# Windowed attention of layer B: from products on VectorE to small matmuls on TensorE, with a new instruction order

## Chip, core and metric

The kernel runs on one core of a Trainium2 chip. Engines: PE (TensorE: matmuls and transposes; its weight loads are shown apart as PEld), DVE (VectorE), ACT (ScalarE), POOL (GpSimd) and SP (SyncE, whose queue issues nearly all transfers). Each engine works through its own instructions in program order and waits for others by semaphores. The metric is the device time of one execution in microseconds, the median of several runs.

## Reference

Four residual layers, A, B, A, B, on 2,048 tokens of width 512, with 32 heads of 16 channels. Layer A is a linear attention with a softmax feature map and isn't changed in what it computes. Layer B is attention over a window: a token attends to itself and to the seven tokens 2, 4, ... 14 places before it.

```python
W, dil = 8, 2
...
pos = jnp.arange(S)
off = jnp.arange(W) * dil
idx = pos[:, None] - off[None, :]
mask = idx >= 0
...
logits = jnp.einsum("bhsd,bhswd->bhsw", q, kg) * scale
logits = jnp.where(mask[None, None, :, :], logits, -1e9)
attn = _softmax(logits, axis=-1)
o = jnp.einsum("bhsw,bhswd->bhsd", attn, vg)
...
x = x + _A_ref(_layernorm(x, axis=-1), A_wqkv, A_w_phi, A_wo)
x = x + _B_ref(_layernorm(x, axis=-1), B_wqkv, B_wo)
x = x + _A_ref(_layernorm(x, axis=-1), A_wqkv, A_w_phi, A_wo)
x = x + _B_ref(_layernorm(x, axis=-1), B_wqkv, B_wo)
```

## The kernel before

**Tiling.** Tokens are cut into four blocks b of 512, each of four tiles t of 128; x stays in the SBUF. Weights are loaded once. A step name says its stage: a1 (keys and values of layer A, and the sum kv over all tokens), a2 (queries), a3 and a4 (denominators, the output of layer A and its projection `s_out`), b1 (Q, K, V of layer B), b2 (scores and softmax), b3 (values, then `s_out`). L is 0 for the first pair of layers and 1 for the second. kv joins all four blocks, so a3 of a layer starts after a1 of all of them.

**Order.** Each stage registers its steps in threads, one for each engine. The text `_ORDER` lists the order in which the steps are issued, for all engines together. `_CHOICE` holds one bit for each eviction (`flex`): DVE (L190) or ACT (L192). In `s_out` the bit also says how x is added: by one more matmul with the identity on PE (L523) and a copy on ACT (L530), or by an addition on DVE (L533). `_SLOTS` gives each tile its buffer. A queue never passes a step that waits.

**Layer B.** b1 makes Q, K and V transposed, channels on partitions (the 384 matmuls of L927), with 16 columns of the block before in front of K and V (copies on POOL). `prod` (L1019, DVE) multiplies Q by the eight shifted windows of K, four times 128x4096 a block; `lgt` (L1026, PE) adds the products of a head with a 0/1 matrix on 128x32 tiles of the array, so that heads and offsets lie on partitions. Exponentials are on ACT (L1033), denominators are matmuls (`den`, L1042) with ln and exp on ACT (L1047, L1049), and DVE multiplies (`PT`, L1054). `vrep` (L988, SP) spreads V over the partitions, 16 transfers a block. `pav` (L1081, DVE) multiplies probabilities by values, four times 128x4096 a block, and `mo` (L1090, PE) adds up the eight offsets with another 0/1 matrix; the result leaves by L190/L192 as oT, and `s_out` (L520) projects it.

**Other lines of the prediction.** L540: squares for the layernorm (ACT). L460 and L451: transposes of the normalized x on PE and by DMA. L668: kv of layer A (128x33 tiles of the array, 64 columns). L714 and L782: sums and denominators of layer A (128x32 tiles, 128 columns). L808 and L816: broadcast of the factors and the multiplication. L900: output of layer A (32x32 tiles, 512 columns). L242 and L252: clearing a constant and building PHI at the start, L493: the first layernorm's statistics.

Of the kernel before, what the change touches and what calls it, by code (L numbers as in the profile page):

```python
# [16 lines left out]
P = 128  # L17
# [12 lines left out]
KVW = 16 + TB  # L30
VGW = 3 * KVW + TB + 8
# [5 lines left out]
_BUFS = {"big": 8, "med": 16, "t2": 6, "ps": 8}  # L37
# [3 lines left out]
    "fold_dma": (),  # L41
    "half_k": ((0, 3), (1, 3)),
    "half_ln": (),
    "split": ((1, 2), (1, 3)),
    "v_dram": (),
    "half_mo": (),
    "rho_pad": 0,
# [10 lines left out]
av 8 i i i i i i i i i i i i 0 f 0 g e 2t 0 bs 9 h a d c 0 j k t i i j l 27 o p 3 3 d6 b 1x 1x t 1y o m 2 2 1q  # L58
1z 1x 1x q u t r 1q v x w n s 1r w 1s 4 20 y 21 1x 22 1x 23 1q 1q 1q 1q 1v 1w z 3d 3d 3d 1u 1t 25 3e 3e 3e z 5
3e 3e z z 26 10 18 18 d5 1 z 16 11 4i 15 6 1h 13 3d 3e 3e 25 25 26 18 25 18 12 26 26 28 26 26 26 26 19 12 28  # L60
2a 28 1h 18 14 12 12 1a 28 1c 3e 2g 2g 1f 2h 2h 1h 1h 1b 1i 2b 1b 1e 1d 29 2j 2k 1h 1j 1n 2r 1b 1l 2s 1b 2c 2r
1k 2s 17 2g 2g 2h 2h 1k 1k 2h 2h 2h 2h 2d 1g 2d 2d 2d 2e 2j 1m 35 36 32 2o 2o 33 2s 33 32 33 33 2r 2s 2s 1o 2o
2o 2d 2r 3a 1k 3a 1p 2p 2o 24 24 2s 24 2u 2v 35 37 2u 2u 2u 2s 2i 2w 2j 3a 2s 3a 2l 2z 2j 24 32 32 34 2m 3b 33
3d 3f 3f 2z 2z 2z 33 2f 33 33 2f 2f 2f 3a 3a 2q 2q 2q 30 3a 2n 3a 3a 2z 3e 2q 2x 35 35 b6 3b 3a 2y 31 31 31 31
3c 3c 38 3c 39 3c 3m 3f 3n 3o 3o 3o 24 24 3g 3g 3g 3f 3p 3q 3g 3g 3g 3g 3g 3r 3q 3f 3g 24 3h 3i 3i 5l 5m 5n 3p
3s 3q 3j 3k 3k 3t 3q 3p 3x 5m 3w 3u 3h 3i 3i 3q 3v 3q 3q 3y 3h 3i 3q 3i 3h 3i 3q 5l 5o 5p 5r 5m 5q 7 7 3z 3q
3i 3j 3k 5m 5l 5s 3k 7 7 5m 5m 5m 3h 3i 7g 40 5u 44 41 42 5t 5m 5m 3j 3j 7h 7i 3k 5v 5m 5w 43 7h 45 7j 45 60
3k 3k 3k 46 45 45 5y 5x 5z 61 61 48 47 47 61 49 47 4a 47 4b 62 47 4b 63 3j 4g 94 4c 45 4d 45 4e 4f 3k 45 45 61
64 63 4h 4p 65 95 7j 7j 66 4q 63 96 95 97 97 63 67 7h 63 67 69 7h 6b 4k 4k 4k 4l 4p 4r 4k 4m 4p 4p 4s 4t 7k 7n
6a 68 6c 4o 7m 50 50 4u 4u 4u 4n 4u 7l 4w 97 7o 7p 7p 7q 7s 3l 4x 7r 7r 7p 7t 7p 6o 7u 50 7r 7r 7v 6o 6j 4v 4y  # L70
4j 6o 6q 6o 4j 4z 6k 6p 6r 6j 7r 6e 6l 95 6d 95 7v 6t 6s 6f 6d 7w 6e 7z 7x 98 9b 9a 99 6g 7y 9c 6e 6j 6j 9d 9d
6u 9d 6e 6n 80 6m 9d 6h 6v 6v 9e 9h 9f 6i 9g 9f 6w 6v 6v 6w 6w 9f 9i 9f 87 88 8h 9j 9f 50 82 9j 9l 6w 6x 6x 87
87 6w 81 83 9n 6x 9k 87 8b 89 51 51 51 51 52 52 8c 8c 8e 6u 6u 6u 9m 8j 8a 8d 8c 6v 6y 3l 8f 82 9o 82 85 82 50
51 52 4z 4z 4z 9q 9q 9s 8c 6z 8g 6y 6z 9r 71 70 6y 6y 6z 6z 72 86 a0 a0 a1 73 84 8i 74 75 74 74 50 74 8i 76 8i
77 a2 76 79 53 53 54 55 54 a5 56 53 54 9v 78 76 9q 9q 76 a0 81 53 9v 9w 9p 7a 57 9v 9u a7 76 7a 9t 8j 7c 9y 54
58 59 59 59 9v 59 9x 7d 7e 5a 8j 8j 7b 7f 5c 5b 5d 5b 5b a0 8k 5e 5b 5f 8k 9z a7 5b 5f 5j 8k 8k 8l a3 5i b4 a4
b7 5h b4 b4 b4 8l 5g b5 b5 a7 b5 b5 a7 8k 8l 8j c3 8i c3 b8 c4 c4 c4 c4 a8 8m a8 a8 a8 c3 a9 a9 5k at c1 b5 a6
8m au au c1 c2 b5 c2 aw c2 c2 a8 a9 b5 b5 8n 8o 8n 8p 8m at au at at 8n 8q 8m a7 aa 8n aw 8r 8s au au au 8s 8s
8t au au 8s 8v a6 a6 8u aa 8w aa 8x 8u 8u 8u 8y ab ac ab ad a6 aa b7 8u b9 b7 c3 8y 90 92 c1 91 c1 c2 8z c2 c2
aw ay ab c2 ba ae ab af aw b0 c4 c4 b1 bc ag ag ag ag ah bc aj ak bc c1 c4 c4 bc al ax c3 ai ai ai bd b1 ai am  # L80
93 bf bi bg az bf ai am ar bf bf bg bg aq b7 bg bg bg bg bg bb an ao ag ag ap bi ag ag b1 b1 bc b2 c2 bi bn bi
bl bk as bq br br bq br br bq bq b1 br by by by by bt b3 b3 b3 b3 br be be be br br bz c5 c5 bh bj bn bn bn c5
bu c4 by by by by c6 bo by c6 c6 c5 bt bt bt bn bv c6 c6 c6 bz be bp bp bw bm bp bp c0 c0 by c6 c6 bx c0 c0 c9
c5 ca c6 cb cb cc cb cd ce cd fr fs c7 c8 c7 c8 c8 ft cc ci cf cd cg cd c7 c8 c8 fs fu c8 e2 fu ch cd e3 cd cc
cj ck e4 cd c7 c8 c8 c7 e3 e2 cm cd c8 e6 e7 fu cl cd cd cn cp co e5 e3 hb e3 cr e2 ea e9 cq hc cs e3 cs e8 e3
e3 hd eb ec e3 e3 e3 ed ct cv hc eh cs he ee cs ef cw eg ei cx ei ei cu ei cu cu cu fs cy fs fv ej cu cy d0 cz
ek d2 fw fx fz d3 cs cs fy cs cs g0 g0 g0 el ek em ek en ek d4 d1 dc g1 eo ek g2 g3 g2 dc de eo es g0 g4 dd dh
g2 g5 g2 he hc eq g6 d7 d8 d7 d7 d7 he di dc g2 dc d9 ep er hc et dn hf da db df dh dh dh hi hh hj hg hk hk hk
dj dk dl dm dm g6 g7 g9 dn dn dg ga f0 f0 hl hm hn hm ho hm ev ew f1 hk dn g8 do do hp f2 fa fc hm hq do do dp
ev ex fc gb ev f0 dp ey dn f3 f0 hm fc f4 hq ev ez fc do dp dn dq dq d6 f5 f6 dm dm eu hs gi gj gi fd gs hr fd  # L90
ht fd hu hv fd dq fe fe f5 f5 f8 f5 f9 f7 fb gk fd fe fc gn gn gp gi gi gl gm gd gd gd ge ic gf i7 i7 i9 gg i8
dr dr dt ds dr du hx hy gd dq gu dr dv gn gq gh i7 ff ia gu fb go ff fg fh fb fb eu gv gc gn i2 gr i3 hx hz hx
i7 i2 ib gv i4 hx i1 gc hw i2 i2 i5 gu i0 gu gv gv gw gt ie fg fi if i6 ie id gw if dw dx id gv gw id id ie ie
if if ig dw ff ig if ig fg fj dw e0 dw ff fg fk ie fl fm fl fn gu fl fl fp ih ih ih ih e1 ii ii ii ik ij fq dy
gt gt gt fo fo il io io io io ii im ip iq ip is ir ir ih ii in ip ip iu it ir gx ir gy gx gx gx gz gy h0 dz dz
iv gy h1 h4 gx gy h2 h4 iw iv h5 h5 h6 h7 gy h4 h3 h5 h8 h9 h7 h7 h4 h5 ha h7
# [4 lines left out]
    "0011111111111001110111111010000010010000000000000001011111101100100000110101000110000010000001110111"  # L101
    "1101011110010000110101000000000000001101011000000000100100000000000000000101111100000011011000000000"
    "0000000000001101111010000000100101011111010000011001110111000000000000000111111011101110010100101000"
    "00000000000001111001000000000000000000000000000000000000000000000000000000000001111"
# [3 lines left out]
_SLOTS = {  # L108
    "big": (
        "0123456701231231456204632073205712053720457604356704213560421356720415763215063506432506"  # L110
    ),
    "med": (
        "0123456789abcdef5837ae98eeaeae471853bc9e43cbe47199ce3185413cebf94c8f74e3581bc71931bc7f370bf9ac21584e"
        "af9c37214a0b589dec37"
    ),
    "t2": (
        "0123450123450342150132451032451032451032451302153421530421503452014520345123045130425123504321504321"
        "5043215043210451023134"
    ),
    "ps": (  # L120
        "0123456701234750613250746132074365462150743510635127035164051362731405263710452763210743562107423251"
        "0764376215043762435107625407152367423167052341760543210675432170652147053624036542076314257603415203"
        "6415026734107534105234065265346053460562036207346201542015471204712603712035764120356471032516407324"
        "6735012463754021637261350247613025476130746513072463501742635017463015276301562703152760432764327014"
        "6570324650324705613245076"
# [4 lines left out]
class _Fast:  # L130

    def __init__(self, ctx, tc, A_x, A_wqkv, A_w_phi, A_wo, B_wqkv, B_wo, out):
        self.tc, self.nc = tc, tc.nc
        self.out = out
        e = ctx.enter_context
        self.const = e(tc.tile_pool(name="const", bufs=1))
        self.bigp = e(tc.tile_pool(name="bigp", bufs=1))
        self.medp = e(tc.tile_pool(name="medp", bufs=1))
        self.t2p = e(tc.tile_pool(name="t2p", bufs=1))
        self.small = e(tc.tile_pool(name="small", bufs=2))  # L140
# [7 lines left out]
        self.ntile = {t: 0 for t in _BUFS}  # L148
        for n in ("xn", "xnT", "oT", "Eq", "rS", "kvp", "K", "QT", "Vg", "PT", "vh"):
            setattr(self, n, {})  # L150
# [7 lines left out]
    def ps(self, dt=F32):  # L158
        return self.psp.tile([P, 2048 // (4 if dt == F32 else 2)], dt, name="ps", tag=self.slot("ps"))
# [35 lines left out]
    def constants(self):  # L195
        nc, const = self.nc, self.const
        self.ident = ident = const.tile([P, P], BF16, name="ident")
# [1620 lines left out]
```

## Time and profile before

| What | Value |
|---|---|
| Median of 3 runs | 329.83 us (329.33 to 331.2) |
| Span of the profiled execution | 327.5 us, 8033 instructions, granted TensorE clock 0.998 |
| PE busy | 310.3 us (95%), 3176 matmul records |
| DVE busy | 302.2 us (92%), 439 instructions |
| ACT busy | 279.3 us (85%), 634 instructions |
| POOL busy | 25.3 us (8%) |
| DMA | 35.41 MB; the hardware queue 53.6% of 16 engines' span |

The span goes from the first instruction to the last of one profiled execution; the page gives no other time for it, and the runs' median is 2.3 us above it. Busy time is the time in which at least one instruction of the engine is under way: instructions overlap at their ends, on ACT and DVE by some 90 ns each, so sums of mean durations exceed it. [...] A few matmul records are missing (234 of 256 of L520 with 128x128 tiles are there, for instance). In a group of the lines view stand: line, engine, operation, output and inputs, shapes and count; then busy us and mean ns of one; then idle time before it and what ended it.

### The profile page before, as it was taken

How to read it: one execution, taken by the hardware profiler on the slowest of the kernel's cores; microseconds unless marked ns; L12 is line 12 of the kernel's file. 1: busy time of each engine (PE TensorE's matmuls, PEld its weight loads, DVE VectorE, ACT ScalarE, POOL GpSimd, SP SyncE). 2: the span in 40 equal slices, each digit the busy share in tenths (PEclk: the TensorE clock that was granted, in tenths of full speed). 3: DMA queues.
4: the chain of work that ended last, by engine and by line, in shares of the span. 5: the costliest groups of instructions: out<-in, count | busy, mean ns of one | idle time of the engine just before them, and what ended most of it. 6: DMA issues, size and time to landing. Idle time of an engine off the chain costs nothing. (4 is left out here: it accounts for less than half of the span.)

```text
span 327.5 us, 8033 instructions
## 1 busy us (share of the span) xinstructions
PE 310.3 (95%) x3176; PEld 149.5 (46%) x3203; DVE 302.2 (92%) x439; ACT 279.3 (85%) x634; POOL 25.3 (8%) x50
## 2 busy tenths in 40 slices
PE   7999999999999999999999999979999999999873
PEld 3655456445444444443444455644544454433221
DVE  7998995998998999899999999699999999999993
ACT  5999988998888999989999999798999996676550
POOL 4000000000021003000000000000000208400000
PEclk9999999999999999999999999999999999999999
DMA  7980000004556899998750300023436977679952
GB/s 197 380 197 3 0 2 4 2 20 120 105 148 135 152 164 133 139 121 154 137 135 1 67 3 2 4 59 90 128 58 125 179 146 134 150 139 158 166 176 92
DMA packets 37388, 35.41 MB, mean 108 GB/s; under 512 B 23008, under 2 KB 32224, under 8 KB 37344
## 3 DMA queue, kind: packets, MB, share of 16 engines
q1 hardware_dynamic: 36816, 34.81, 53.6%
q8 instruction: 27, 0.44, 0.6%
q14 instruction: 17, 0.14, 0.2%
q10 hardware_dynamic: 528, 0.02, 0.1%
HBM read 10.50 MB, written 2.36 MB: 39 GB/s over the span
## 5 line engine op out<-in xcount | busy, mean ns | idle before, releaser
L927 PE MATMUL ps<-xnT,WB 128*128 128x512 bf16 x384 | 87.6, 380 | 0.5 <-DMA xnT<-xn 0.5
L1081 DVE TENSOR_TENSOR pav<-PT,Vg 128x4096 bf16<-128x4096 bf16 (+1 forms) x34 | 72.0, 2162 | 1.5 <-DMA Vg<-V 1.0
L1019 DVE TENSOR_TENSOR prod<-QT,K 128x4096 bf16<-128x4096 bf16 x32 | 72.5, 2291 | 0.3 <-ACT QT L192 0.2
L927 PEld LDWEIGHTS <-WB 128*128 128x128 bf16 x384 | 42.3, 114 | 43.3 <-issue 5.8
L520 PEld LDWEIGHTS <-oT 128*128 128x128 bf16 x256 | 23.8, 97 | 34.5 <-ACT oT L192 5.7
L192 ACT CAST oT<-ps 128x512 bf16<-128x512 f32 (+1 forms) x60 | 32.1, 587 | 8.4 <-PE ps L1090 7.1
L706 ACT ACTIVATE Eq<-ps 128x512 bf16<-128x512 f32 x64 | 34.0, 615 | 0.7 <-PE ps L698 0.6
L520 PE MATMUL ps<-WoB,oT 128*128 128x512 bf16 x122 | 32.1, 380 | 2.4 <-ACT oT L192 2.0
L599 ACT ACTIVATE Ek<-ps 128x512 bf16<-128x512 f32 x64 | 33.6, 622 | 0.4 <-PE ps L593 0.2
L698 PE MATMUL ps<-xnT,WA 128*128 128x512 bf16 x128 | 30.7, 380 | 0.6 <-DVE Eq L816 0.6
L540 ACT ACTIVATE sqd<-x 128x512 bf16<-128x512 bf16 x48 | 30.1, 643 | 1.0 <-DVE x L533 0.8
L605 PE MATMUL ps<-WA,xnT 128*128 128x512 bf16 x120 | 30.0, 380 | 0.5 <-issue 0.2
L593 PE MATMUL ps<-WA,xnT 128*128 128x512 bf16 x124 | 29.7, 380 | 0.6 <-DMA xnT<-xn 0.2
L520 PE MATMUL ps<-WoA,oT 128*128 128x512 bf16 x120 | 29.2, 380 | 0.4
L533 DVE SCALAR_TENSOR_TENSOR x<-ps,x 128x512 bf16<-128x512 f32 x38 | 25.4, 686 | 1.9 <-PE ps L520 1.7
L192 ACT CAST V<-ps 128x512 bf16<-128x512 f32 x31 | 17.5, 595 | 4.4 <-PE ps L927 4.3
L192 ACT CAST K<-ps 128x512 bf16<-128x512 f32 x31 | 17.8, 585 | 3.7 <-PE ps L927 3.3
L530 ACT ACTIVATE x<-ps 128x512 bf16<-128x512 f32 x26 | 15.1, 598 | 6.4 <-PE ps L523 6.3
L192 ACT CAST QT<-ps 128x512 bf16<-128x512 f32 x29 | 17.1, 592 | 2.5 <-PE ps L927 2.5
L651 DVE TENSOR_TENSOR Ek<-Ek,rk 128x4096 bf16<-128x4096 bf16 (+1 forms) x10 | 18.6, 1858 | 0.5 <-ACT rk L646 0.5
L593 PEld LDWEIGHTS <-xnT 128*128 128x128 bf16 x128 | 12.1, 97 | 15.4 <-DMA xnT<-xn 0.7
L446 ACT ACTIVATE xn<-x,nmr,rstd 128x512 bf16<-128x512 bf16 x23 | 18.2, 822 | 1.0 <-DVE nmr L435 0.8
(129 smaller groups left out, 433.3 us busy)
## 6 DMA issues: line engine op xcount, KB each, us to landing
Vg<-V SPq DMA_DIRECT2D x128, 131.5 KB, 4.4
Prho<-rd SPq DMA_DIRECT2D x8, 512.0 KB
x<-in_A_x_dram SPq DMA_DIRECT2D x3, 512.0 KB
WB<-in_B_wqkv_dram SPq DMA_DIRECT2D x3, 512.0 KB, 11.6
wraw<-in_A_wqkv_dram SPq DMA_DIRECT2D x4, 256.0 KB, 4.5
out_dram<-x SPq DMA_DIRECT2D x4, 256.0 KB, 2.2
out_dram<-x SPq DMA_DIRECT2D x8, 128.0 KB, 2.2
x<-in_A_x_dram SPq DMA_DIRECT2D x4, 128.0 KB
```

Source lines behind the costliest of these rows:

```text
L192: self.nc.scalar.copy(out=out, in_=in_)
L520: nc.tensor.matmul(y[:], lhsT=oT[:, c, t * P:(t + 1) * P], rhs=Wo()[:, c, :], start=(c == 0), stop=(c == NB - 1 and not onpe))
L533: nc.vector.scalar_tensor_tensor(out=xb[:, t, :], in0=T[t][:], scalar=1.0, in1=xb[:, t, :], op0=ALU.mult, op1=ALU.add, **kw)
L540: nc.scalar.activation(out=sqd[:], in_=xb[:, t, :], func=ACT.Square, accum_out=T["ss"][:, t:t + 1])
L593: nc.tensor.matmul(pk[:], lhsT=xnT[:, t, k, :], rhs=self.WA[:, k, D:2 * D], start=(k == 0), stop=(k == NB - 1))
L599: nc.scalar.activation(out=T["E"][:, t, s, :], in_=T["k", t][:], func=ACT.Exp, scale=1.0 - 2.0 * s)
L605: nc.tensor.matmul(pv[:], lhsT=xnT[:, t, k, :], rhs=self.WA[:, k, 2 * D:3 * D], start=(k == 0), stop=(k == NB - 1))
L698: nc.tensor.matmul(pq[:], lhsT=self.WA[:, k, hb * P:(hb + 1) * P], rhs=xnT[:, :, k, :], start=(k == 0), stop=(k == NB - 1))
L706: nc.scalar.activation(out=self.Eq[L, b][s][:, :, hb, :], in_=T[hb][:].rearrange("p (t i) -> p t i", t=4), func=ACT.Exp, scale=1.0 - 2.0 * s)
L927: nc.tensor.matmul(pp[:], lhsT=self.WB[:, k, i * D + c:(i + 1) * D:NB], rhs=xnT[:, :, k, :], start=(k == 0), stop=(k == NB - 1))
L1019: nc.vector.tensor_tensor(out=pr[:], in0=QT[:, c:c + 1, :].to_broadcast([P, NW, TB]), in1=win, op=ALU.mult)
L1081: nc.vector.tensor_tensor(out=pv, in0=PT[:, :, lo:lo + n].unsqueeze(1).to_broadcast([P, NB, 2, n]), in1=vw, op=ALU.mult)
```

## The change

Layer B is computed in another way; layer A keeps its operations, some of them twice as wide.

- *Tokens* are laid out anew in x: a block's tile t holds tokens of one parity (r = t // 2), so that the window is eight neighbours. Loads and stores of x follow.
- *b1* keeps its 384 matmuls: Q and K transposed as before, V with tokens on partitions. Q is copied by eight transfers a block (`qsc`) into `Qbd`, which holds, for each group of four heads, a block diagonal with zeros elsewhere. V goes with a column of ones into `Vs`, is written to DRAM (`vwr`, 2 a block) and read back (`vrd`, 8 a block) into `Vbd`, block diagonal too. `Qbd` and `Vbd` exist once; their zeros are set at the start by DVE.
- *b2*, for each tile of 128 tokens: scores of 32 keys against 40 queries for four heads at once, on 64x32 tiles of the array; exponential of 640 elements twice; a band mask on DVE.
- *b3*, for each tile: probabilities as weights, values as moving data (68 columns: four heads of 16 and a one), 32 matmuls and 32 for the keys of the group of 32 before; ln and exp of the denominator on ACT; the division by DVE straight from PSUM.
- *b4*: the output is transposed, by DMA for blocks 0 to 2 and on PE for block 3, then `s_out`.
- PSUM is one tile of eight banks; `pp` takes two neighbouring banks. Exponentials of a1 and a2, the evictions of a4 and the multiplication of a3 work on two banks at a time. ln and exp that were one step are two.
- `_ORDER`, `_CHOICE` and `_SLOTS` are new throughout: 1551 steps instead of 1452. 3 residual additions are done by the identity on PE instead of 26. Unused options are gone.

```diff
+WN = 40
+DV = DH + 1
...
+    "ob_dma": {(0, 0): 4, (0, 1): 4, (0, 2): 4, (1, 0): 4, (1, 1): 4, (1, 2): 4},
...
     def ps(self, dt=F32):
-        return self.psp.tile([P, 2048 // (4 if dt == F32 else 2)], dt, name="ps", tag=self.slot("ps"))
+        bank = self.PS[:, int(self.slot("ps")[2:]), :]
+        return bank if dt == F32 else bank.bitcast(dt)
+
+    def pp(self):
+        k = int(self.slot("pp")[2:])
+        return self.PS[:, k:k + 2, :]
...
+        self.Qbd = const.tile([P, NB, NB, TB], BF16, name="Qbd")
+        self.Vbd = const.tile([P, 2, 9, NB, 8 * DV], BF16, name="Vbd")
...
+        def zero_q(i):
+            nc.vector.memset(self.Qbd[:, 2 * i:2 * i + 2, :, :], 0.0)
+
+        def zero_v(i):
+            nc.vector.memset(self.Vbd[:, i // 2, 5 * (i % 2):5 + 4 * (i % 2), :, :], 0.0)
...
-        for b in range(1, 4):
-            add("ld_x%d" % b, "SP", lx, b)
+        for b in range(1, 4):
+            for r in range(2):
+                add("ld_x%d" % b, "SP", lx, b, r)
...
-            nc.scalar.activation(out=T["E"][:, t, s, :], in_=T["k", t][:], func=ACT.Exp, scale=1.0 - 2.0 * s)
+            nc.scalar.activation(out=T["E"][:, 2 * t:2 * t + 2, s, :], in_=T["k", t][:], func=ACT.Exp,
+                                 scale=1.0 - 2.0 * s)
...
+        def mv(t):
+            xnT = self.xnT["B%d" % L, b]
+            T[2, t] = pp = self.ps()
+            for k in range(NB):
+                nc.tensor.matmul(pp[:], lhsT=xnT[:, t, k, :],
+                                 rhs=self.WB[:, k, 2 * D:3 * D],
+                                 start=(k == 0), stop=(k == NB - 1))
...
+        def qsc(g):
+            lo = DH * g
+            nc.sync.dma_start(out=self.Qbd[lo:lo + DH, :, g % 4, :], in_=T[0][lo:lo + DH, :, :])
...
+        def vrd(r, c):
+            j = 0 if b else 1
+            src = self.VD[L][r, 256 * b - 32 + 32 * j:256 * b + 256, c * 8 * DV:(c + 1) * 8 * DV]
+            nc.sync.dma_start(out=self.Vbd[32 * c:32 * c + 32, r, j:9, c, :],
+                              in_=src.rearrange("(j k) e -> k j e", k=32))
...
+        def mm(S, r, c, s, n, pos, K, k0, q0):
+            o = S[32 * c:32 * c + 32, r, s * 160 + pos:s * 160 + pos + 1]
+            out = bass.AP(o.tensor, o.offset, [list(o.ap[0]), [WN, NB], [1, n]])
+            nc.tensor.matmul(out, lhsT=K[64 * r:64 * r + 64, c, k0:k0 + 32],
+                             rhs=Q[64 * r:64 * r + 64, c, :, q0:q0 + n],
+                             start=(s == 0 and pos == 0), stop=(s == 1), tile_position=(64 * r, 32 * c),
+                             skip_group_check=True)
+
+        def sc(f):
+            S = T[f] = self.pp()
+            K = self.K[L, b]
+            for s in range(2):
+                k0 = t * P + 64 * f + 32 * s
+                for c in range(NB):
+                    for r in range(2):
+                        mm(S, r, c, s, 32 if f and s else WN, 0, K, k0, k0)
+            if f == 0:
                 return
...
+            for c in range(NB):
+                for r in range(2):
+                    mm(S, r, c, 1, 8, 32, Kp, k0, t * P)
+
+        def ex(f):
...
+            nc.scalar.activation(out=E, in_=T[f][:, :, 0:320], func=ACT.Exp, scale=float(DH) ** -0.5,
+                                 accum_out=self.stE[:, 2 * idx + f:2 * idx + f + 1])
+
+        def msk():
+            E = self.ET[L, b, t][:].rearrange("p r s h q -> p (r s h) q")
+            nc.vector.tensor_tensor(out=E, in0=E, in1=self.maskW[:].unsqueeze(1).to_broadcast([P, 32, WN]),
+                                    op=ALU.mult)
...
+        def pv(e, s, n, ks, pos):
+            j = 4 * (t % 2) + 1 + s - (pos > 0)
+            v = V[:, t // 2, j, 0, DV * e:DV * e + 1]
+            rhs = bass.AP(v.tensor, v.offset, [list(v.ap[0]), [8 * DV, NB], [1, DV]])
+            nc.tensor.matmul(T["O"][32 * s:32 * s + n, e, 0:NB * DV],
+                             lhsT=self.ET[L, b, t][:, e // 4, ks, e % 4, pos:pos + n], rhs=rhs,
+                             start=(e % 4 == 0 and pos == 0), stop=(pos > 0),
+                             tile_position=(0, 32 * s), skip_group_check=True)
+
+        def mo():
+            T["O"] = self.pp().rearrange("p o (e x) -> p (o e) x", x=P)
+            for e in range(8):
+                for s in range(4):
+                    pv(e, s, 32, s, 0)
+            for e in range(8):
+                for s in range(4):
+                    if s or t % 2 or b:
+                        pv(e, s, 8, (s + 3) % 4, 32)
...
+        def ln():
+            T["r"] = self.sm([8, NB], "rdB")
+            den = T["O"][:, :, 0:NB * DV].rearrange("p e (c d) -> p e c d", d=DV)[:, :, :, DH]
+            nc.scalar.activation(out=T["r"][:], in_=den, func=ACT.Ln, bias=self.tiny_t[:, 0:1])
+
+        def rd():
+            nc.scalar.activation(out=T["r"][:], in_=T["r"][:], func=ACT.Exp, scale=-1.0,
+                                 accum_out=self.stR[:, idx:idx + 1])
+
+        def nrm():
...
+            nc.vector.tensor_tensor(out=out, in0=num, in1=T["r"][:].unsqueeze(3).to_broadcast([P, 8, NB, DH]),
+                                    op=ALU.mult)
...
+        def tr(lo, n):
+            nc.sync.dma_start_transpose(
+                out=tile()[:, lo:lo + n, :, :].rearrange("k t c p -> k (t c) p"),
+                in_=self.oB[L, b][:, lo:lo + n, :].rearrange("p t d -> p (t d)"))
```

In the new list DVE begins with kvT, maskH, PHI, half of Qbd's zeros, the small constants, indAV, a quarter of Vbd's zeros and indB, and then the statistics of the first two tiles.

More of the change, by code (lines that the diff above doesn't have):

```diff
@@ L63 @@
[L63 to L67, printed above, removed]
@@ L126 @@
+    "et": (
+        "01234560231460512436015263142501"
     ),
@@ L275, in ind_b @@
                 in_=self.indAV[:].rearrange("p (a h) -> p a h", h=8).unsqueeze(3).to_broadcast([P, NB, 8, DH]))
-        def ind_den():
-            nc.vector.tensor_copy(out=self.indDen[:],
-                                  in_=self.indAV[:].unsqueeze(1).to_broadcast([P, NB, H]))
-        for f in (zero, small, mask_h, phi, ind_s, mask_2, ind_qk, ind_av, ind_b, ind_den):
+        for f in (zero, small, mask_h, phi, ind_s, mask_2, ind_av, ind_b, mask_w):
             add("c_" + f.__name__, "DVE", f)
+        for i in range(2):
+            add("c_zq%d" % i, "DVE", zero_q, i)
+        for i in range(4):
+            add("c_zv%d" % i, "DVE", zero_v, i)
         def warm():
@@ L572, in s_out @@
                 add(st, "ACT", sq, t)
-                if half and t % 2:
-                    norm(t - 1, 2)
             elif last and split:
@@ L578, in s_out @@
                 add(st, "SP", store, t - 1, t + 1)
-        if not last and not half:
+        if not last:
             norm(0, 4)
@@ L640, in t1, with rl @@
                                     op=ALU.add)
+        def rl(t, m):
+            s1 = T["s1"][:, 0:m * G]
+            nc.scalar.activation(out=s1, in_=s1, func=ACT.Ln)
         def rr(t, m):
@@ L990, in s_b1 @@
-        if b:
-            add(st + "v", "POOL", vhalo_in)
-        else:
-            add(st + "k", "POOL", kzero)
-            add(st + "v", "POOL", vzero)
-        for i in range(3):
-            for c in range(NB):
-                add(st + "qkv"[i], "PE", mm, i, c)
-                self.flex(st + "qkv"[i], ev, i, c)
-        if b:
-            add(st + "kh", "POOL", halo)
-        if b < 3:
-            add(st + "v", "POOL", vhalo_out)
-        if (L, b) in _OPT["v_dram"]:
-            add(st + "v", "SP", vwr)
@@ new lines, in vrd @@
+        def vrd(r, c):
[3 more added lines that the diff above has]
+                              in_=src.rearrange("(j k) e -> k j e", k=32))
+        for i in range(2):
+            for c in range(NB):
+                add(st + "qk"[i], "PE", mm, i, c)
+                self.flex(st + "qk"[i], ev, i, c)
+        for g in range(8):
+            add(st + "q", "SP", qsc, g)
@@ new lines, in s_b3 @@
+    def s_b3(self, L, b, t):
+        nc, add = self.nc, self.step
+        st = "b3_%d%d%d" % (L, b, t)
+        key = "A%d" % (L + 1)
+        idx = (L * 4 + b) * 4 + t
+        T = {}
+        V = self.Vbd
+        def pv(e, s, n, ks, pos):
[23 more added lines that the diff above has]
+        def nrm():
+            if (L, b) not in self.oB:
+                self.oB[L, b] = self.med([4, D], "oB")
+            num = T["O"][:, :, 0:NB * DV].rearrange("p e (c d) -> p e c d", d=DV)[:, :, :, 0:DH]
+            out = self.oB[L, b][:, t, :].rearrange("p (c e d) -> p e c d", c=NB, d=DH)
+            nc.vector.tensor_tensor(out=out, in0=num, in1=T["r"][:].unsqueeze(3).to_broadcast([P, 8, NB, DH]),
+                                    op=ALU.mult)
+        add(st, "PE", mo)
+        add(st, "ACT", ln)
+        add(st, "ACT", rd)
+        add(st, "DVE", nrm)
```

566 lines of the change are left out of this document (234 added, 332 removed).

## The prediction

> **What bounds the kernel now.** I read the windows view first (busy time of each engine in stretches of 20 us), to see who is full where.
>
> ```profile
> 100.00:120.00 20.00, 19.95 (x166) 9.04 (x167) 19.38 (x20) 18.03 (x45) 1.46 (x2) 1.00 0.88 146
> 260.00:280.00 20.00, 20.00 (x138) 9.46 (x136) 19.91 (x13) 16.46 (x34) 7.18 (x4) 1.00 0.75 137
> 300.00:320.00 20.00, 16.59 (x136) 5.65 (x137) 19.37 (x21) 10.04 (x20) 0.00 (x0) 1.00 0.82 172
> 320.00:328.00 8.00, 2.16 (x16) 0.69 (x8) 2.56 (x4) 0.37 (x1) 0.00 (x0) 0.90 0.23 75
> ```
>
> The columns are PE, PEld, DVE, ACT, POOL. PE and DVE are both full in layer B; only in the last 28 us does PE have holes, and there DVE is full. But a matmul's record is longer than its turn, so I went on to the chain of waits, whose pieces are cut from start to start.
>
> ```profile
> 251.50 0.86 PE ps L520 x4
> 252.37 1.84 PE ps L1026 x32
> 254.21 4.44 PE ps L927 x20
> 258.65 0.43 PE ps L1042 x2
> 259.08 2.59 PE ps L927 x12
> ```
>
> A full-array matmul of 512 columns takes 2.59/12 = 0.216 us, and the chain stays on PE without a gap. So TensorE really is the bound between the ends, with DVE close behind. The 32 matmuls of L1026 run four at a time on 128x32 tiles: 8 turns of 0.216 = 1.73, measured 1.84; the 20 after them should take 4.32 and take 4.44. Going into a tiled block and out of it costs 0.11 + 0.12 us. What a small tile costs is in PE's timeline:
>
> ```profile
> 50.25 2.15 PE L668 MATMUL ps<-Ek,vaug 128*33 128x64 bf16 x128
> 52.33 1.04 PE L698 MATMUL ps<-xnT,WA 128*128 128x512 bf16 x4
> 54.38 0.63 PE L782 MATMUL ps<-Eq,ZM 128*32 128x128 bf16 x32
> 54.84 1.02 PE L714 MATMUL ps<-Eq,indS 128*32 128x128 bf16 x32
> ```
>
> L668 (64 columns, two tiles) needs 52.33 - 50.25 = 2.08 us; less 0.21 for the two changes that is 14.6 ns a matmul, 29 ns a turn. L782 (128 columns, four tiles) needs 0.46 us for 32: 14.4 ns each, 57 ns a turn. Turns of 29, 56 and 216 ns at 64, 128 and 512 columns lie on one line: 0.417 ns a column plus 2.5 ns, shared by as many matmuls as there are tiles. Weight loads don't show in it.
>
> **What the change removes and adds on PE.** The old list, written out as steps, changes the tile shape of PE 109 times, the new one 128 times.
>
> ```profile
> L1019 DVE TENSOR_TENSOR prod<-QT,K 128x4096 bf16<-128x4096 bf16 x32 | 72.5, 2291 | 0.3 <-ACT QT L192 0.2
> L1081 DVE TENSOR_TENSOR pav<-PT,Vg 128x4096 bf16<-128x4096 bf16 x30 | 67.5, 2288 | 1.5 <-DMA Vg<-V 1.0
> L1026 PE MATMUL ps<-prod,indQK 128*32 128x512 bf16 x256 | 16.4, 381 | 1.7 <-DVE prod L1019 1.7
> L1090 PE MATMUL ps<-pav,indAV 128*32 128x512 bf16 x240 | 16.1, 382 | 1.2 <-DVE pav L1081 1.1
> L523 PE MATMUL ps<-x,ident 128*128 128x512 bf16 x26 | 9.9, 379 | 0.0
> ```
>
> Removed: 256 matmuls of lgt, 64 turns of 0.216 = 13.8; those of mo in b3 the same (60 turns, and 8 of 0.109) = 13.8; 16 of den = 3.5; and, because the new choices leave 3 of the 26 residual additions by identity on PE (L523), 23 x 0.216 = 5.0. Sum 36.1.
>
> Added: scores. Each of 32 steps has 24 matmuls of 160 columns, 8 of 128 and 8 of 32 on eight 64x32 tiles: three turns of 69, one of 56, one of 16 ns = 0.28 us; 32 x 0.28 = 9.0. Values: 32 + 32 matmuls of 68 columns on four tiles, 16 turns of 31 ns = 0.49 us; 32 of them 15.7. Transposes: the last block of each layer turns its output on PE, 32 x 0.056 = 1.8. Sum 26.5. Changes of tile shape: 19 x 0.11 = 2.1. The projections, layer A and the folds keep their matmuls. **PE net -7.5 us.**
>
> No row has eight tiles of 64x32, nor four with 68 columns, so the 7.5 ns for each of these 3,296 matmuls are extrapolated. The nearest rows lie at 13.5 to 14.6 ns (L900: 16 tiles share 216 ns; L782; L668), and the line explains them all by columns alone. Bounds: the line, 24.7 us in all, and the dearest row, 14.6 x 3,296 = 48 us, 23 more. I take the line, since within one turn of L714 the records of loads and matmuls start 2 to 4 ns apart.
>
> [...]
>
> **The other engines.** DVE loses 72.5 + 72.3 (prod, pav) + 5.4 (PT). It gains the mask, 32 x 0.82 (between 0.687 at 1,024 and 1.22 us at 2,048 elements) = 26; the division 32 x 0.69 = 22; 39 more evictions of Q, K, V at 0.69 = 27; 23 more residual additions at 0.67 = 15; memsets 7. Net about -53 of 302. ACT loses 34 oT and 39 Q/K/V evictions and 23 residual copies (about 0.55 each with their overlap, 53), old exponentials and denominators (25), and about 6 by exponentials twice as long; it gains 64 exponentials of 640 elements (0.6 + 0.1 + 0.21 - 0.16 overlap = 0.75; 48), and 32 ln/exp pairs with a read (0.6; 19). Net about -17. Both are hidden behind PE, the only full engine afterwards; without that cover ACT alone would still need some 262 us, so none of this is on the path between the ends. POOL's halo copies go and cost nothing either way.
>
> **SP and the single buffers.** Here new waits arise. 128 Vg transfers become 64 qsc, 16 vwr and 64 vrd, and six DMA transposes come on top.
>
> ```profile
> 247.26 5.01 SPq L988 DMA_DIRECT2D Vg<-V  x8
> 253.35 2.98 SPq L451 DMA_TRANSPOSE xnT<-xn  x1
> ```
>
> An issue takes 5.01/8 = 0.63 us of SP, a transpose 2 to 3. Qbd exists once: the 8 qsc of a block wait for the last score matmul of the block before; behind them on SP stand vwr, vrd and a transpose, for which the values wait. The next scores come after 8 x 0.63 = 5.0 us of issue plus landing, 2.2 (x tiles) to 4.4 us (Vg): 7.2 to 9.4. In the new list PE has between these points projections and value blocks worth 7.2 to 11 us. The cover just suffices, and I book 0 (bounds: -2, as DVE and ACT wait less; +15, below).
>
> **The head.** The first statistics now stand behind PHI, two memsets and indB on DVE.
>
> ```profile
> 0.94 0.27 DVE L242 MEMSET kvT<- 128x256 uint32 x1 [0.94 <-PEq L1802]
> 3.41 0.69 DVE L493 BATCH_NORM_STATS2 stat<-x 128x6 f32<-128x512 bf16 x1
> 6.39 0.66 DVE L252 TENSOR_TENSOR PHI<-phis,maskH 128x512 bf16<-128x512 bf16 x1
> ```
>
> 256 words take 0.27 us, so half of Qbd (2,048 words) about 1.8 and a part of Vbd (1,088) about 1.0. PHI needs phis (issued 0.84, 2.4 us to land), so it ends near 3.9; with the memsets, indAV and indB the first statistic starts near 7.9 instead of 3.41. PE has nothing but the warm-up to hide that: +5.0 (bounds 0 to +6).
>
> **The tail.** Now PE is idle or waiting for about 13 us between 280 and the end (stream time of its matmuls against the clock). After: from the last block's first value step the chain is mo 0.6, ln and exp 0.75, nrm 0.69, four of them overlapped 5.6, then transpose and copy 1.3, eight matmuls 1.9, residual 0.7 and 4.6 from there to the end of the span (322.9 to 327.5 now): 14.1 us, with 8 us of PE work in it, and 1.5 us before it for the eight vrd. Idle 7.6: **-5.3** (bounds -9 to 0).
>
> **Sum.** -7.5 + 0 + 5.0 - 5.3 = -7.8: span 327.5 to 319.7. The runs' median 329.83 lies 2.3 above the profiled span; kept, this gives 322.
>
> **Rivals.**
> 1. *Slack pays more.* The waits outside head and tail (about 7 us, half of them at 200 to 218 where layer A's sums are joined) and the head's delay are absorbed since DVE and ACT have 50 to 70 us free: another -5 to -16, so 317 to 306, about 312. For it: those waits end on DVE and ACT. Against: the chain there is one of dependences.
> 2. *SP gates layer B (slower).* One mechanism: Qbd's reload. If its issue plus landing exceeds PE's cover at the six handovers inside layers by 2.5 us, PE loses 15: 337. It decides from a reload of about 9.5 us on, that is, when landings take 4.4 us as Vg's do. For it: Vg's landing. Against: the heavy Vg transfers, which fill the DMA engines to 0.8 in this stretch, are gone.
> 3. *Small matmuls cost 14.6 ns.* +23: 345.
> 4. *Tiles of the new shapes don't run beside each other.* Each start takes a turn as narrow as L668's, 29 ns: 3,296 x 0.029 = 96 us, +71: 393. Against: L668's two tiles and L782's four share their turns.
> 5. *No net change.* The tail gains nothing, since the round trip of V through DRAM ends it: 327 to 331, about 328.5.
>
> **How the numbers follow.** Forecast 0.42, rival 1 0.25, rival 2 0.15, rival 3 0.07, rival 4 0.01, rival 5 0.10. 0.5% of 329.83 is 1.65 us, about what this measurement can tell from none. Faster (under 328.2): 0.40 of the forecast, 0.25, 0.03 of rival 5: 0.68. Same: 0.02 + 0.07 = 0.09. Slower: 0.23. The forecast's own range is 316 to 328; to hold 8 in 10 it takes in rival 1 below (306) and rival 2 above (337).
>
> **What would show it.** Right: 64 value matmuls of a step within about 0.5 us start to start and 16 score matmuls of 160 columns in 0.14; PE without gaps in layer B; the first statistic near 8 us; the last residual to the end 4.6 us. Wrong: PE waiting for qsc at each block (rival 2), value steps of 0.9 us (3), or a first statistic still near 3.4 us.

## The result, and the profile after

The changed kernel takes 370.13 us (median of 4 runs, 368.38 to 372.28) beside 329.86 for the kernel before: a ratio of 1.1214, 95% interval 1.1161 to 1.1268. It is slower by 40 us; the forecast was 322, and the range ended at 337. The profiled execution spans 369.7 us (327.5 before) with 13,641 instructions (8,033 before).

The windows view of after, in the columns of the table shown before (us, PE, PEld, DVE, ACT, POOL, granted clock, DMA share, GB/s):

```profile
100.00:120.00 20.00, 17.96 (x110) 7.83 (x110) 14.60 (x32) 13.58 (x31) 0.00 (x0) 1.00 0.84 182
260.00:280.00 20.00, 15.54 (x117) 6.11 (x118) 13.85 (x28) 11.66 (x27) 0.00 (x0) 0.91 0.67 122
300.00:320.00 20.00, 17.48 (x539) 9.64 (x527) 10.52 (x16) 14.42 (x42) 0.00 (x0) 1.00 0.74 121
340.00:360.00 20.00, 16.23 (x468) 9.69 (x472) 12.66 (x19) 10.18 (x30) 0.00 (x0) 0.83 0.48 127
```

PE had 19.95 of 20 us from 100 to 120 and 20.00 from 260 to 280; now it has holes in each of these stretches, while DVE and ACT have eased to between 10 and 15. No engine is full: PE is still the busiest, but waits are added to its work. And a column that stood at 1.00 before now falls: the granted clock.

The page of after, its rows on TensorE's clock and on the queue that brings instructions, and the shares of the chain of waits by engine:

```profile
PEclk9699999969999989999999999989999999999967
...
q8 instruction: 49, 0.80, 0.9%
...
PE 57%; DMA 14%; DVE 12%; ACT 7%; issue 7%; SPq 1%; DVEq 0%; ACTq 0%
```

Before, the clock's row held forty nines, and q8 brought 27 packets, 0.44 MB. The chain of before can be followed back only to 219.08 us (26% of the span PE, 3% DVE, 2% ACT, 1% issue, no DMA), the chain of after to 0.77, so their shares can't be set side by side; within its stretch the chain of before has no DMA. Three things have changed at once: half clock in seven stretches (a 6 is a slice in part at half speed), 22 packets of instructions more, and waits for DMA and for "issue", that is, for nothing that the profile shows. The view of waits, PE's own lines, names them (us in total, times, the longest):

```profile
PE PS L1029 <- issue: 12.5, 8, 2.6
PE PS L884 <- DVE Eq L853: 6.4, 3, 3.4
PE PS L471 <- DVE xn L455: 3.0, 1, 3.0
PE PS L1119 <- DVE okb L1115: 1.9, 1, 1.9
PE PS L884 <- DVE Eq L834: 1.9, 2, 1.1
PE PS L1029 <- DMA Vbd<-vd: 1.8, 2, 1.4
PE PS L596 <- DMA xnT<-xn: 1.5, 1, 1.5
```

All of PE's lines of this view add up to 10.1 us before and 39.0 after: issue 0.4 to 17.2, DVE 5.2 to 17.2, DMA 1.1 to 4.1, ACT 3.4 to 0.5.

**Where the issue waits sit.** PE's timeline of after, a stretch with scores (L975), projections (L910) and values (L1029):

```profile
124.77 0.46 PE L975 MATMUL PS<-Qbd,K 64*32 64x160 bf16 x31
125.16 1.90 PE L910 MATMUL PS<-xnT,WB 128*128 128x512 bf16 x8
126.99 0.51 PE L975 MATMUL PS<-Qbd,K 64*32 64x160 bf16 x40
127.52 0.71 PE L1029 MATMUL PS<-Vbd,et 128*32 128x68 bf16 x56
128.16 2.76 PE L910 MATMUL PS<-xnT,WB 128*128 128x512 bf16 x12
130.85 1.83 PE L1029 MATMUL PS<-Vbd,et 128*32 128x68 bf16 x169
134.88 0.30 PE L1029 MATMUL PS<-Vbd,et 128*8 128x68 bf16 x15 [2.20 <-issue]
```

A run of values goes at full speed for some 170 matmuls and then stops for 2.20 us, in the middle of a step, waiting for nothing that the profile shows. Counting PE's instructions in the trace (a weight load and its matmul are two, and PE's semaphore instructions count as well) puts ten such stops at the same place, 193 or 194 past a multiple of 256. A q8 packet is 0.80 MB / 49 = 16 KB; the stops fit 256 instructions a packet, and so do the 22 more packets for some 5,500 more weight loads and matmuls. The trace's DMA records tie the two together: each of the ten stops ends 1.2 to 1.6 us after a q8 packet has landed. So PE ran dry between packets: the ten stops last 15.9 us from start to start (before, no stop at such a place is longer than 0.31 us).

**An account that fits.** From the clock's records I took the time in which PE works at half clock (gaps between starts counted up to 0.45 us); half of it is lost, since full matmuls start 0.427 us apart there (21 in after) instead of 0.216 (841). Span less waits less that half leaves a rest:

| Kernel | Span | PE's waits | lost to half clock | rest |
|---|---|---|---|---|
| before | 327.5 | 10.1 | 0.0 | 317.4 |
| after | 369.7 | 39.0 | 13.5 | 317.2 |

The 42.2 us of span are 28.9 of waits and 13.5 of clock, less 0.2 of rest. This is bookkeeping, not yet a cause: waits can stand in for each other. The experiments take them one by one; their rows of this table come below.

### The profile page after: what moved, and what is told of

It is laid out like the page before. It is cut to its first block, busy times and chain, and to the rows that moved or that the text cites. A ratio compares the mean times of both kernels' runs of the same rounds, so it can differ in the third digit from the quotient of the medians.

```text
span 369.7 us, 13641 instructions
## 1 busy us (share of the span) xinstructions
PE 321.9 (87%) x5918; PEld 168.7 (46%) x5964; DVE 262.1 (71%) x505; ACT 261.1 (71%) x597; POOL 5.4 (1%) x26
## 4 chain that ended last, share of the span: by engine, by line
PE 57%; DMA 14%; DVE 12%; ACT 7%; issue 7%; SPq 1%; DVEq 0%; ACTq 0%
PE PS L910 11%; PE PS L530 9%; DMA Prho<-rd 8%; PE PS L709 6%; PE PS L1029 6%; PE PS L596 5%; PE PS L609 5%; PE PS L917 4%; PE PS L975 3%; DVE Eq L834 2%; PE PS L675 2%; DMA xnT<-xn 1%; PE PS L884 1%; DMA Vbd<-vd 1%; ACT sqd L550 1%
## 5 line engine op out<-in xcount | busy, mean ns | idle before, releaser
L910 PE MATMUL PS<-xnT,WB 128*128 128x512 bf16 x256 | 63.0, 391 | 0.7 <-DVE K L202 0.6
L1004 ACT ACTIVATE et<-PS 128x640 bf16<-128x640 f32 x64 | 44.4, 702 | 12.3 <-PE PS L975 12.1
L543 DVE SCALAR_TENSOR_TENSOR x<-PS,x 128x512 bf16<-128x512 f32 x61 | 40.8, 684 | 6.1 <-PE PS L530 5.9
L910 PEld LDWEIGHTS <-WB 128*128 128x128 bf16 x256 | 24.3, 100 | 30.9 <-issue 5.4
L1029 PE MATMUL PS<-Vbd,et 128*8 128x68 bf16 (+1 forms) x2016 | 23.1, 198 | 14.3 <-issue 12.5
L717 ACT ACTIVATE Eq<-PS 128x1024 bf16<-128x1024 f32 x32 | 30.7, 1020 | 4.3 <-PE PS L709 4.2
L530 PE MATMUL PS<-WoA,oT 128*128 128x512 bf16 x121 | 31.7, 398 | 0.9 <-issue 0.4
L602 ACT ACTIVATE Ek<-PS 128x1024 bf16<-128x1024 f32 x32 | 30.9, 1034 | 1.6 <-PE PS L675 0.9
L596 PE MATMUL PS<-WA,xnT 128*128 128x512 bf16 x121 | 29.6, 382 | 2.2 <-DMA xnT<-xn 1.5
L530 PE MATMUL PS<-WoB,oBT 128*128 128x512 bf16 x117 | 30.2, 391 | 1.2 <-issue 0.9
L917 PE MATMUL PS<-WB,xnT 128*128 128x512 bf16 x113 | 29.7, 384 | 1.6 <-issue 0.9
L609 PE MATMUL PS<-WA,xnT 128*128 128x512 bf16 x122 | 30.5, 379 | 0.4 <-issue 0.2
L709 PE MATMUL PS<-xnT,WA 128*128 128x512 bf16 x128 | 30.1, 379 | 0.2 <-DVE Eq L834 0.2
L1029 PEld LDWEIGHTS <-et 128*8 128x8 bf16 (+1 forms) x2016 | 19.6, 91 | 21.0 <-issue 15.8
```

Source lines behind the costliest of these rows:

```text
L530: nc.tensor.matmul(y[:], lhsT=lhs(t, c), rhs=Wo()[:, c, :], start=(c == 0), stop=(c == NB - 1 and not onpe))
L543: nc.vector.scalar_tensor_tensor(out=xb[:, t, :], in0=T[t][:], scalar=1.0, in1=xb[:, t, :], op0=ALU.mult, op1=ALU.add, **kw)
L596: nc.tensor.matmul(pk, lhsT=xnT[:, t, k, :], rhs=self.WA[:, k, D:2 * D], start=(k == 0), stop=(k == NB - 1))
L602: nc.scalar.activation(out=T["E"][:, 2 * t:2 * t + 2, s, :], in_=T["k", t][:], func=ACT.Exp, scale=1.0 - 2.0 * s)
L609: nc.tensor.matmul(pv[:], lhsT=xnT[:, t, k, :], rhs=self.WA[:, k, 2 * D:3 * D], start=(k == 0), stop=(k == NB - 1))
L709: nc.tensor.matmul(pq, lhsT=self.WA[:, k, hb * P:(hb + 1) * P], rhs=xnT[:, :, k, :], start=(k == 0), stop=(k == NB - 1))
```

## The experiments

Theory: the new matmuls are as cheap as forecast, and what is lost is (a) instructions that arrive too slowly for runs of small matmuls, (b) the low clock that follows the holes, (c) an order that leaves transfers uncovered. Rivals: the small matmuls cost more than forecast; the loss is head and tail.

**1. Two memsets out of the head.** zero_q(1) ("i") and zero_v(1) ("k") move behind the first statistics, to about 90 us.

```diff
-8 a b 0 cw 2c 2y n n n i n n n n n n n 9 e k n n n 0
+8 a b 0 cw 2c 2y n n n n n n n n n n 9 e n n n 0
...
-86 40 4c 87 88 49 89 a5 a5 h 65
+86 40 4c 87 88 49 89 a5 a5 i k h 65
```

> Only the places of two DVE steps differ: the memset of half of Qbd (1.77 us twice) and the one of a part of Vbd (0.96) go from ahead of the first statistics to where DVE waits for Prho (near 90 us). Theory head: in the changed kernel TensorE stood 3.18 us at 6.90 us for the first transposes, and the low clock from 9.3 to 16.1 us came behind that pause (3.4 us lost); so the first statistic starts near 4 us and the run is 4 to 8 us shorter, 362 to 366. Rival: what follows waits for the loads of x and of the weights anyway, and the time stays within 2 us of 370.

Measured: 365.97 us, 4.2 less; ratio to before 1.1081 (1.1026 to 1.1136). DVE's timeline, first of after, then of this run:

```profile
4.49 1.76 DVE L287 MEMSET Qbd<- 128x2048 uint32 x1 [0.38 <-issue]
...
6.73 0.96 DVE L290 MEMSET Vbd<- 128x1088 uint32 x1 [0.17 <-issue]
7.61 0.36 DVE L296 COPY indB<-indAV 128x512 bf16<-128x512 bf16 x1
7.89 0.68 DVE L504 BATCH_NORM_STATS2 stat<-x 128x6 f32<-128x512 bf16 x1
```

```profile
4.51 0.43 DVE L294 COPY indB<-indAV 128x512 bf16<-128x512 bf16 x1
4.85 0.69 DVE L502 BATCH_NORM_STATS2 stat<-x 128x6 f32<-128x512 bf16 x1
```

The statistic comes 3.04 us sooner, and half clock from 9.26 to 16.09 us, which followed PE's wait of 3.02 us for it, is gone: the first matmul of L609 (L607 here) starts at 14.73 instead of 19.29, 4.6 us sooner. The moved memsets are not free at their new place, where PE now waits for DVE in a way that after does not:

```profile
PE PS L915 <- DVE x L541: 3.5, 1, 3.5
```

The 4.2 us are the balance. The head is worth about what the forecast gave it, and explains a tenth of the 40 us.

**2. The matmuls by themselves.** A block of matmuls whose results nobody uses is put into after ahead of L675's sums: 24 full, 512 of the values' shape, 24 full, 256 of the scores' width, 24 full. It adds work.

```diff
+        full(24)
+        small(512, 68)
+        full(24)
+        small(256, 160)
+        full(24)
```

> The changed kernel with a block of extra matmuls ahead of the first sum of layer A, where no DMA is busy and nothing is waited for: 24 full matmuls, 512 of the value shape (68 columns, four tiles in turn), 24 full, 256 of 160 columns on the same four tiles, 24 full; their results are never used. Theory fetch: instructions come to TensorE's queue in packets of 256 (128 matmuls with their weight loads), and a packet is usable some 2.5 to 4 us after the one before was begun. Then the 512 need not 512 x 8.2 ns = 4.2 us but 9 to 12, in flat stretches of 8 ns a matmul with three or four gaps of 1 to 3 us, all of them at the same place of the queue modulo 256 (193, as the ten gaps of the changed kernel); the 256 of 160 columns (17 ns each by columns, 2.2 us for a packet) have gaps under 1.8 us or none. Rival: the gaps of the changed kernel are waits for ET or Vbd that the profile doesn't show, or pauses of the throttle; then the 512 take 4.2 us without a gap.

Measured (403.36 us, one run); PE's timeline of the block, L1169 the full ones and L1174 the small ones:

```profile
47.75 5.34 PE L1169 MATMUL PS<-WA 128*128 128x512 bf16 x24
53.02 1.67 PE L1174 MATMUL PS<-WA 128*32 128x68 bf16 x181
56.92 1.22 PE L1174 MATMUL PS<-WA 128*32 128x68 bf16 x128 [2.23 <-issue]
60.38 2.00 PE L1174 MATMUL PS<-WA 128*32 128x68 bf16 x128 [2.23 <-issue]
63.83 1.27 PE L1174 MATMUL PS<-WA 128*32 128x68 bf16 x75 [1.45 <-issue]
65.43 6.96 PE L1169 MATMUL PS<-WA 128*128 128x512 bf16 x23 [0.33 <-issue]
72.32 2.94 PE L1174 MATMUL PS<-WA 128*32 128x160 bf16 x157
```

This run settles the most. The 512 take 12.1 us (53.02 to 65.10), as by the theory, where the rival had 4.2. 128 matmuls, 256 instructions with their loads, run in 1.22 us and then wait 2.23: from 56.92 to 60.38 and from there to 63.83 it is 3.46 and 3.45 us a packet, though the second was worked off more slowly. The stops end 1.36 us after a q8 packet has landed, and next to nothing else is moved (DMA share 0.02 from 54 to 66). Long runs of small matmuls thus go at 3.46/128 = 27 ns each, though each costs under 10 ns. The third run of 128 takes 2.00 instead of 1.22, and the 24 full matmuls behind take 6.96 instead of 5.34: the records show half clock from 58.89 to 69.13, right behind the holes (after has none from 16.09 to 74.11). No input was waited for, so the stops are the supply's, and the low clock came behind nothing but such stops.

**3. Another order, by the steps' own durations.** The same steps, re-ordered by laying their traced durations end to end; no instruction more or less. (Orders run to 40 lines of codes and are not shown; the diff of experiments 3 to 6, 8 and 9 is the text of `_ORDER` and `_SLOTS` alone.)

> The changed kernel's own steps, engines and work; only the order of the list and the slots drawn differ. The order was worked out by laying the steps' durations of the trace end to end with their waits, with the rule that TensorE can't begin a packet of 256 instructions sooner than 3.9 us after the one before. That sum gives 357 for the order of the changed kernel (measured span 369.7, with some 10 us lost at the low clock, which the sum leaves out) and 328 for the new one. Theory: the 42 us were lost by the order (fetch gaps, Prho without cover, head, tail), not by the new work; so 330 to 342, fetch gaps under 4 us in sum, TensorE's stream 284 us as before. Rival: the new work itself costs it (matmuls of small tiles, or DVE and ACT as bound); then over 355 in any order.

Measured: 367.1 us, ratio 1.1124 (1.1053 to 1.1195). The expectation missed, and the time lies where the rival had it. PE's waits in this run:

```profile
PE PS L1027 <- issue: 9.0, 7, 2.5
PE PS L908 <- DMA xnT<-xn: 4.4, 2, 2.3
PE PS L915 <- DMA xnT<-xn: 4.0, 1, 4.0
```

The 3.9 us a packet was my estimate: experiment 2 has 3.46, and in after no two packets start less than 3.40 us apart. The sum let transfers land in fixed times. On the chip the transpose (xnT) issued 7.5 us behind Prho's pair landed after 7.25 us. In after two transposes were issued behind a pair of Prho, too, and landed after 4.96 and 7.91 us; the other seven took 4.3 to 5.4. The longest wait, 4.0 us, is for a transpose that stood behind Vbd's loads on SP and was issued only at 114.68, so Prho is a part of it alone. DMA waits went from 4.1 to 12.4 us, while issue waits fell only from 17.2 to 12.4: what the order won was given back in the queue of transfers.

**4. An order without the rule on packets, first try.**

> As e3_order, but the order was worked out without the rule on packets: by the sum without the rule it takes 325, with it 336 (12 us of gaps, part of them hidden in other waits). Theory fetch: 6 to 12 us slower than e3_order, 338 to 350, with gaps of TensorE at place 193 modulo 256 of its queue, over 8 us in sum. Rival (no such rule): no slower than e3_order, up to 3 us faster.

Its order cleared a part of Vbd behind the first load into it, so that the denominators were zero and the kernel ran its second, general path for them: 924.72 us, which says nothing on the question. Experiment 6 asks the same with that step in its place.

**5. An order that knows packets, queueing transfers and the clock.** The steps' durations are laid end to end as in experiment 3, but transfers queue behind each other, packets come at a set rate and TensorE's clock falls by a set rule. That rule was my assumption; no run shows it (experiment 10).

> Again the changed kernel's own steps, engines and work in another order. e3_order lost its gain to transfers: transposes that were issued behind Prho's 512 KB landed after 7.25 us instead of 4.3, and the loads of the next weights after 12. [...] Theory (the loss is order, not work): 328 to 345. Rival (the new work needs its time in any order, as e3_order seemed to say): over 355.

Measured: 347.83 us, ratio 1.0515 (1.0454 to 1.0576): 22.3 us less than after, by order (and the buffers drawn with it) alone. It lies just above the theory's range and well under the rival's 355. Its page and its view of waits:

```profile
PEclk9999999969999999999999999989999999978999
```

```profile
PE PS L308 <- DVE kvT L252: 3.3, 1, 3.3
PE PS L1027 <- DMA Vbd<-vd: 3.2, 5, 1.1
PE PS L1027 <- issue: 3.0, 2, 2.5
```

The issue waits at the values fell from 12.5 to 3.0 us, and Prho's multiplication (L851 here) is no longer among PE's waits.

**6. The same search without the rule on packets.** The search differs from that of experiment 5 by the one rule; the orders that the two found differ in many places.

> [...] Theory fetch: 8 to 14 us slower than e5_order2, with gaps at place 193 modulo 256 of TensorE's queue, 8 us or more in sum. Rival: as fast as e5_order2 or up to 2 us faster.

Measured: 353.56 us, ratio 1.0696 (1.0641 to 1.0752): 5.7 us more than experiment 5. Stops at a packet's place that end with a packet's arrival are 10.1 us (seven) instead of 4.5 (three), 5.6 more. The size is under what was expected (8 to 14), the sign and the link hold. This is the nearest to a price for the packets: about a microsecond of time for a microsecond of stops. It isn't a clean one, since other waits differ too (PE's waits for DMA are 7.3 us instead of 5.5, the loss to half clock 5.8 instead of 7.3).

**7. Without the 992 halo matmuls of the values.** The keys of the group before are left out of the output.

```diff
-            for e in range(8):
-                for s in range(4):
-                    if s or t % 2 or b:
-                        pv(e, s, 8, (s + 3) % 4, 32)
```

> The changed kernel without the second half of the value step: the 992 matmuls of the halo positions are left out (numerators and denominators lack those positions), all else and the order stay. Theory fetch: a value step is 64 instructions instead of 128, so two or three steps in a row no longer eat a packet before the next has come: beside the 992 x 8.2 ns = 8.1 us of stream, most of the 15.8 us of gaps go, some of it into other waits: 14 to 22 us shorter, 348 to 356. Rival (only columns count): 8 us shorter or less, 362 to 366.

Measured: 356.36 us (two runs), ratio 1.0803 (1.0739 to 1.0868), 13.8 less than after, just short of the theory's 14 to 22 and past the rival's 8; at 7.5 ns each the matmuls are worth 7.4. Stops between packets went from 15.9 to 3.9 us and packets from 49 to 41. But the view of waits shows where half of that went:

```profile
PE PS L884 <- DVE Eq L853: 7.5, 3, 3.4
PE PS L975 <- DMA Qbd<-Qs: 6.1, 5, 2.2
```

Qbd and Prho come no sooner, so a PE that gets its instructions earlier waits for them instead. In after's order the stops hide other waits; removed alone they are worth some 6 us, not 12.

**8. The end.** The two squares of the bound (L424, 1.9 us each on ACT), which stand last in the chain of waits, move to where ACT has room.

> Only the two squares of WA on ACT (1.95 us each, the last two steps of ACT ahead of the final test) move: one to ACT's idle time near 103 us, the other to near 162. Theory tail: in the changed kernel they ended the chain (358.6 to 362.5, after the last matmul of the last block), so 2.5 to 4 us shorter, 366 to 367.6. Rival: the stores and the last residual end later anyway, within 1 us of 370.

Measured: 369.61 us, ratio 1.1232 (1.1175 to 1.1289): no change, as the rival had it. The profile's chain ends there, yet the runs do not get shorter.

**9. A third order, with a harsher rate of packets.** The search let packets come more slowly than the 3.46 us of experiment 2; the order is set against that of experiment 5.

> The kernel after with a third order of the same steps: only the text of the order and the slots differ, no instruction is added or left out. [...] Theory (the loss against the forecast is an order that starves TensorE of instructions and of full windows; a better order wins part of it back): 336 to 344, gaps in front of waitless instructions under 4 us in all, half clock in no more windows than there (347.83 measured). Rival (the fifth experiment already has what order can give, and the rest is paid per instruction, wherever it stands): 345 to 350.

Measured: 348.08 us, ratio 1.0579 (1.0555 to 1.0602): nothing won against experiment 5, as the rival said, and the theory's 336 to 344 missed. The profiled execution (344.0 us of span), the shortest of the four, has full clock up to its last 4 us; its waits are 25.1 us instead of 22.1, spread over many small ones:

```profile
PEclk9999999999999999999999999999999999999997
```

So the low clock can nearly be had back by order (the other three executions were granted 0.985 to 0.992), and what is then left is waits.

**10. A hole filled.** 14 full matmuls in the hole from 271.73 to 275.10, in front of half clock at 275.50: if the hole brings it, it should be gone, and the other stretches should stay.

```diff
+            if j == 1164:
+                self.fill()
```

> The kernel after, with 14 full matmuls of 512 columns (3.0 us, result unused, written into a free bank) ahead of the first of the two output steps of layer A's second-layer block 3, where TensorE stands still for 3.37 us from 271.73 on, waiting for the multiplication by Prho on VectorE. Everything behind shifts by 28 instructions in PE's queue. [...] Rival (the low clock comes at fixed distances or from something other than TensorE's own filling): half clock again near 275 to 279. The whole time stays within 4 us of 370 either way, since the later waits for instructions fall elsewhere.

Measured: 365.19 us (one run). Half clock stood at 11.98, 87.08 and 134.86 and at the end; it is gone at 275, but also at 74 and 245, where nothing was changed, and new at 87. In after and here all stretches of half clock begin on one grid of 3.41 us, and the grid doesn't keep its place from run to run (9.26 and 135.55 in after, 11.98 and 134.86 here), so one run can't show that the filling did it: inconclusive. How far standing still decides it also stays open: by PE's busy time, half clock began in after behind windows of this grid in which PE stood still for 31% to 94%, but not behind others with 33% to 58%.

**The account over all runs.** Each row from one profiled execution:

| Kernel | Span | PE's waits (issue) | lost to half clock | rest |
|---|---|---|---|---|
| 1, head | 364.3 | 37.8 (16.6) | 9.6 | 316.9 |
| 3, order | 365.2 | 37.1 (12.4) | 7.7 | 320.4 |
| 5, order | 346.6 | 22.1 (5.4) | 7.3 | 317.2 |
| 6, no packet rule | 353.1 | 29.6 (10.5) | 5.8 | 317.7 |
| 7, no halo | 356.1 | 37.2 (5.8) | 9.2 | 309.7 |
| 8, end | 365.4 | 36.7 (14.5) | 9.5 | 319.2 |
| 9, order | 344.0 | 25.1 (7.5) | 0.0 | 318.9 |
| 10, fill | 363.4 | 35.2 (15.3) | 5.1 | 323.1 |

The rest stays at 317 to 320, but for 7, which has 7.4 us of matmuls less, and 10, which has 3.0 more. So order moves waits and clock and, within some 3 us, nothing else. With the 10.1 us of waits of the kernel before and full clock, the new kernel would come to 317.2 + 10.1 = 327.3 of span, the same as before. By this estimate an order would have to wait less than the kernel before does in order to beat it; none that was run comes near.

## Why the prediction was wrong, by its own steps

- **The bound.** "TensorE really is the bound between the ends" was right for before. That it would stay so ("PE, the only full engine afterwards") was wrong: PE waits 39 us, and the chain of waits runs through DMA, DVE and ACT as well.
- **The price of the new matmuls** held. The prediction took 7.5 ns for each of 3,296; from 127.52 to 128.16, less 0.11 for the change of shape, 64 values (56 of them recorded) take 0.53 us, 8.3 ns each; 32 scores of 160 columns take 0.28 (124.77 to 125.16, less 0.11). A whole score step of 40 takes 0.42 instead of 0.28 (126.99 to 127.52), which is at most 32 x 0.14 = 4.5 us for all. Rivals 3 and 4 (14.6 and 29 ns each by their shapes) fall. Yet 27 ns a matmul is what long runs come to, for another reason.
- **PE net -7.5.** The matmuls' columns bear it out: by 0.417 ns a column and 2.5 ns a turn, PE's stream is 291.5 us before and 281.7 after, with 12.5 and 14.7 us for 109 and 128 tile changes of 0.115: -7.6. The rest of the account shows none of it (317.4 and 317.2). The dearer score steps (at most 4.5 us) and an end that is 3.5 us longer would about take it back; that they do is not shown.
- **DVE and ACT.** Forecast about 249 and 262 us, measured 262.1 and 261.1. Both were off the path as engines, but not as links: PE's waits for DVE rose by 12 us.
- **SP and the single buffers, booked at 0.** PE's waits for all DMA are 4.1 us against 1.1. Rival 2 (337, Qbd's reload gates layer B) didn't happen in after; it begins to in experiment 7, where Qbd costs 6.1 us once the stops are gone.
- **The head, +5.0,** with the statistic near 7.9 us: 7.89, and experiment 1 got 4.2 us back from the two memsets.
- **The tail, -5.3.** Nothing came: from the end of the last residual to the end of the span it is 8.1 us (361.58 to 369.7) instead of 4.6, half clock begins at 350.59, and 2.60 us of the last block's values are a stop between packets.
- **The step that failed** is the sum's middle: "-7.5 + 0", the 0 resting on "the cover just suffices". It asked only whether Qbd's transfers are covered. It had no term for the supply of instructions, though the change adds 5,608 of them; it took the clock as fixed at the 0.998 of before; and of layer A it said that its operations are kept, and didn't price that the new order takes away the work that covered Prho's round trip through DRAM. That trip is about as long as before (6.2 to 9.3 us from issue to landing in the first pair of layers, 6.1 to 10.1 in after). Before, neither PE nor DVE waits for it; in after DVE waits 8.8 us for Prho and PE 6.4 for the product, and the chain of waits has

```profile
75.89 9.56 DMA Prho<-rd
...
94.88 10.09 DMA Prho<-rd
...
263.24 10.56 DMA Prho<-rd
```

How the 40 us divide among the three can't be said as a sum, since they cover for each other: removed by order together, 22 us come back (experiment 5); the packets are worth about 6 (experiments 6 and 7, neither of which changes them alone), the head 4. What the low clock alone costs is known from the account only, since no run removed it by itself. The 18 us that are left of the best order are 12 more of waits than before and 7 of half clock by its account; experiment 9 did not get below it, so whether a better order exists stays open.

## What to carry to other kernels

Before trading a few wide instructions for thousands of small ones, count the instructions of each engine and compare the work between them with the time that a packet of 256 takes to arrive (3.46 us here): short runs between wide matmuls went at full speed here (64 values in 0.53 us), long ones did not (27 ns a matmul in experiment 2), so they should be spread among wide matmuls. When the order is new throughout, list the round trips that the old order covered and check each one's cover again, with the delay of transfers issued behind others (some 4 us for the second of a pair of Prho here). Holes on TensorE can cost twice: half clock was seen behind many of them (13.5 us lost in after, by the account), though not behind all.

## What the runs showed of the hardware

**Instructions come in packets of 256, one in 3.46 us in a long run** (experiment 2, 128 loads and 128 matmuls a packet, 2.23 us of standing still in each; in after no two packets start less than 3.40 us apart). Ten stops between packets take 15.9 us in after.

**Half clock is seen behind holes of at most 3.4 us.** In after PE's longest wait is 3.37 us, and still 36 us of the span are at half clock, in stretches of 3.41 and 6.83 us but for the last; the 24 full matmuls behind the stops of experiment 2 took 6.96 instead of 5.34. That the holes bring it about fits all runs but was not shown by taking one away (experiment 10).

**Transfers issued close behind others land later.** Of a pair of Prho in after (512 KB each), the second lands some 4 us behind the first: 6.1 to 6.5 and 9.6 to 10.1 us after their issue in the first pair of layers. A transpose issued behind such a pair took 7.25 us (experiment 3), 4.96 and 7.91 (after), the others of after 4.3 to 5.4.
